# Two transformer layers on one core: the fold's slabs in buffers of their own, no fold ahead of sums that open a group, and a pause of six units behind the token split

## The chip, the cores and the metric

The kernel runs on one core of a Trainium2 chip. The metric is the device time of one execution in microseconds (us). Names of engines follow the profile: PE is TensorE (matrix products), PEld its weight loads, DVE is VectorE, ACT is ScalarE, POOL is GpSimd, and SP is SyncE, whose queue issues nearly all DMA transfers here.

## What is computed

The reference applies two blocks A and B twice, with the same weights, to 2048 tokens of 576 features in fp32. There are 32 heads of 18 features.

```python
def _A_ref(x, wq, wk, wv, wo):            # attention, one K and V for all heads
    q = (x @ wq).reshape(B, S, H, Dh).transpose(0, 2, 1, 3)
    k = x @ wk;  v = x @ wv
    p = softmax(einsum("bhqd,bkd->bhqk", q, k) * Dh ** -0.5)
    return einsum("bhqk,bkd->bhqd", p, v).transpose(...).reshape(B, S, H * Dh) @ wo

def _B_ref(x, wqkv, w_phi, wo):           # linear attention with learned features
    q, k, v = ...x @ wqkv...
    pq, pk = einsum("bhsd,hdf->bhsf", q, w_phi), einsum("bhsd,hdf->bhsf", k, w_phi)
    phi_q = concat([softmax(pq), softmax(-pq)]);  phi_k = the same of pk
    kv = einsum("bhsf,bhsd->bhfd", phi_k, v);  z = sum of phi_k over the tokens
    return ((phi_q @ kv) / (phi_q @ z + 1e-6)).reshape(B, S, D) @ wo

x = x + _A_ref(_layernorm(x), ...);  x = x + _B_ref(_layernorm(x), ...)   # twice
```

## The kernel before

The tokens are cut into 16 tiles of 128. A layer (A then B) has a **loop** in which the attention scores are computed and, beside them, most of B for the tiles that are already through A. Between the two loops, and after the second, stands a **tail** in which the rest of B is done. The first loop has work that the second lacks: the weights of B's keys and queries are first multiplied with `w_phi`, head by head, which is called the fold (`fold_phi`).

**The loop** (`attend`). A *group* is one tile of queries with half of the heads; there are 32 groups per layer. A *unit* is two score products against 128 keys (L518 on PE, into a tile `sc`) and one exponential of 1024 columns (L994 on ACT, from `sc` into `pt`). `sc` has three buffers, so PE can be three units ahead of ACT. Two units make one tile of sums (L806 on PE: `pt` times `vst`, added up over 16 tiles in an accumulator). PE runs in bursts: `scores(3)`, then either one piece of other work or two to three tiles of sums; when there is nothing else to do, the loop goes in steps of two units. Whether a piece is taken is decided while the program is written, by a credit that grows by a fixed pace per burst.

**Two accumulator banks.** One PSUM bank of the tiles `ps` and `acc` holds the running group's sums, the other one ("spare") serves all other work, one *bankful* at a time. When a group opens (its first tile of sums), the two change roles: the new sums go where the last bankful was, and the old sums are read by DVE in `finish_group` (L908, L912, L913, L916, L133, L134: six instructions in a row) before the bank can serve as spare.

**The other work** comes from the generator `stream`, by kind:
- kind F, the fold, ten slabs of `wqkv`: two sorts of transposes (L350, and L337 for the last 72 columns) that DVE copies out (L351, L338), and two sorts of products (L355, L360), which DVE copies out too (L357, L362). The slab comes by DMA (L332) into a buffer `wstage` out of three, which `load_weight` (L168, L165) uses as well for the weights that DVE splits into a high and a low part (L133, L134).
- kind P, a product of 14 matmuls (L240): two for the output projection (with `wdhi`, `wdlo`), two each for B's keys (`wahi`, called K here), values and queries. DVE evacuates a K bankful with L551 and four more instructions.
- kind U, the state update (L595, 32 small matmuls; DVE adds them with L601).

After U a tile's features are finished on DVE: `feature_end` twice (L563, L564, L565) and a transposition (L647). At the same moment the next tile's tokens are split (`turn_tokens`: L133, L134, L673, L674), and its K bankfuls may begin.

The order of PE and of DVE in the loop is the order in which the program is written (`in_order` pins it); SP's and ACT's order is chosen by the scheduler under the same dependencies. Each engine works strictly in its order.

Of the kernel before, what the change touches and what calls it, by code (L numbers as in the profile page):

```python
# [9 lines left out]
F32 = mybir.dt.float32  # L10
# [9 lines left out]
P = 128  # L20
S = 2048
D = 576
H = 32
DH = 18
NT = S // P
# [36 lines left out]
def kernel(ctx, tc, x_in, wq, wk, wv, wo, wqkv, w_phi, wob, out):  # L62
    nc = tc.nc
# [4 lines left out]
    stage = ctx.enter_context(tc.tile_pool(name="stage", bufs=3))  # L68
# [67 lines left out]
    def row_slot(src, k, cols):  # L136
        if k < 4:
            return [(slice(0, P), src[k * P : (k + 1) * P, cols])]
        return [(slice(0, 64), src[512:576, cols]), (slice(64, P), src[512:576, cols])]
# [112 lines left out]
    def bankful(kind, ps, shape=(P, HALF)):  # L252
        yield Kind(kind)
        return ps.tile(list(shape), F32, name="ps")
# [54 lines left out]
    def fold_phi(ps, tmp):  # L309
        room = tmp("bd")  # L310
        rows = room[:, : KT * DH].rearrange("p (k d) -> p k d", d=DH)
        flat = w_phi.rearrange("h d f -> (h d) f")
        nc.sync.dma_start(rows[:126, 0:4, :], flat[0:504].rearrange("(g p) f -> p g f", p=126))
        nc.sync.dma_start(rows[:72, 4, :], flat[504:576])
        bd = room[:, KT * DH : KT * 8 * DH].rearrange("p (k j d) -> p k j d", j=7, d=DH)
        for j in range(7):
            V.tensor_scalar(bd[:126, 0:4, j, :], rows[:126, 0:4, :], mask18[:126, j : j + 1],
                            None, op0=ALU.mult)
            if j < 4:
                V.tensor_scalar(bd[:72, 4, j, :], rows[:72, 4, :], mask18[:72, j : j + 1],  # L320
                                None, op0=ALU.mult)
        yield STAGE
        wt, fo = tmp("wt"), tmp("fo")
        units = [(half, k) for half in (1, 0) for k in range(KT)]

        def fetch(n):
            if n == len(units):
                return None
            half, k = units[n]
            st = stage.tile([P, D], F32, name="wstage")  # L330
            for r, part in row_slot(wqkv, k, slice(half * D, (half + 1) * D)):
                nc.sync.dma_start(st[r, :], part)  # L332
            return st

        def short(pl, st):
            if st is not None:
                T.transpose(pl[:72, :P], st[:, 504:576], idf)  # L337
                V.tensor_copy(wt[:72, 512:640], pl[:72, :P])  # L338

        st = fetch(0)  # L340
        yield STAGE
        yield STAGE
        pl = yield from bankful("F", ps, (P, P))
        short(pl, st)
        yield -110
        for n, (half, k) in enumerate(units):
            following = fetch(n + 1)
            pt = yield from bankful("F", ps, (P, 4, P))
            for g in range(4):
                T.transpose(pt[:126, g, :], st[:, g * 126 : (g + 1) * 126], idf)  # L350
            V.tensor_copy(wt[:126, 0:512], pt[:126].rearrange("p a b -> p (a b)"))  # L351
            yield -440
            po = yield from bankful("F", ps, (P, 504))
            for g in range(4):
                T.matmul(po[:, g * 126 : (g + 1) * 126], wt[:126, g * P : (g + 1) * P],  # L355
                         bd[:126, g].rearrange("p a b -> p (a b)"), start=True, stop=True)
            V.tensor_copy(fo[:, :504], po)  # L357
            yield -880
            pl = yield from bankful("F", ps, (P, 2 * P))
            T.matmul(pl[:, P : P + 72], wt[:72, 512:640],  # L360
                     bd[:72, 4, :4, :].rearrange("p a b -> p (a b)"), start=True, stop=True)
            V.tensor_copy(fo[:, 504:D], pl[:, P : P + 72])  # L362
            short(pl, following)
            nc.sync.dma_start(scratch[half, k * P : (k + 1) * P, :], fo[:, :D])
            st = following
            yield -330

    kst = const.tile([P, S], F32R, name="kst")
# [277 lines left out]
    def block_transpose(blocks, src, dst, pause=0):  # L646
        V.transpose(blocks, src)  # L647
        for _ in range(pause):
            yield
        for q in range(P // 32):  # L650
            rows = slice(q * 32, (q + 1) * 32)
            nc.sync.dma_start(dst[:, rows].rearrange("(b f) t -> f b t", f=32),
                              blocks[rows, :].rearrange("f (b t) -> f b t", t=32))
            yield
# [22 lines left out]
    def mix(i, xs, st, ps, spill, loads, slow, after):  # L677
# [7 lines left out]
        blocks = bw.tile([P, NKG, P], F32, name="pht").rearrange("p a b -> p (a b)")  # L685
        spilling = block_transpose(blocks[:, : 2 * D], eq.rearrange("p h s d -> p (h s d)"), spill[i], SPILL)
        next(spilling)
# [192 lines left out]
    def attend(layer, st, a1o, stream):  # L880
# [13 lines left out]
        with ctx1:  # L894
# [36 lines left out]
            def values(c, g, t, pt):  # L931
                if t == 0:
                    homes.reverse()
                    acc[c, g] = bank(*homes[0], [P, CW])
                add_values(acc[c, g], t, [pt[j // 2][:, j % 2, :] for j in range(GH)], t == 0, t == NT - 1)
                if t == NT - 1 and (c, g) == groups[-1]:
                    st["last"] = acc[c, g]
                elif t == NT - 1:
                    finish(c, g)
# [8 lines left out]
            def tick():  # L948
                ticks[0] += 1
                for queue in (urgent, loads, slow):  # L950
                    if queue and next(queue[0], DONE) is DONE:
                        queue.popleft()

            kind, credit, paused = [None], [0.0], [False]
# [32 lines left out]
            units = [(n, t, hh) for n in range(len(groups)) for t in range(NT) for hh in range(2)]  # L987
            pts, at, done = {}, [0], [0]
# [54 lines left out]
            def sums(until):  # L1043
                while done[0] < until:
                    n, t, _ = units[2 * done[0]]
                    values(*groups[n], t, [pts.pop((n, t, hh)) for hh in range(2)])
                    done[0] += 1
                    in_order()

            def earn(count):  # L1050
                credit[0] = min(credit[0] + st["pace"] * count / BURST, 2)

            def burst():
                ready = scores(BURST)
                tick()
                earn(BURST)
                work = peek()
                held = at[0] + BURST - 2 * done[0]
                if work == "P" and credit[0] >= 1 and not paused[0] and held <= TILES:
                    fill()  # L1060
                    credit[0] -= 1
                    paused[0] = True
                else:
                    paused[0] = False
                    if work == "F" and credit[0] >= 1:
                        fill()
                        credit[0] -= 1
                    count = 3 if credit[0] + st["pace"] >= 1 else 2
                    sums(min(ready, max(done[0] + count, -(-(at[0] + BURST - TILES) // 2))))
                    if work == "U":  # L1070
                        fill()
                    tick()

            while at[0] < len(units):
                if not st["idle"]():
                    burst()
                else:
                    ready = scores(2)
# [13 lines left out]
    BURST = 3  # L1092
    TILES = 9
    DUE = 9
    SPILL = 4
    PACES = ((0.6, 0.44), (0.39, 0.39))
    FLIP = 84
    TAIL = 100
# [18 lines left out]
    st = {"late": [], "norms": const.tile([P, NT // PAIR], F32, name="norms"), "wq": weight_tiles("b")}  # L1117
# [27 lines left out]
    with first, tc.tile_pool(name="ps0", bufs=7, space=PSUM) as ps:  # L1145
# [27 lines left out]
        pair, following = ([first_tile(i) for i in range(k, k + PAIR)] for k in (0, PAIR))  # L1173
# [46 lines left out]
    for layer in range(LAYERS):  # L1220
        last = layer == LAYERS - 1
        st.update(start_state(bw), added=set())
        with tc.tile_pool(name="a1o", bufs=2) as a1o:
# [11 lines left out]
            def stream(v, layer=layer):  # L1235
# [3 lines left out]
                unflipped, st["left"] = deque(), list(range(NT))  # L1239
                st["closed"], st["pace"] = -1, PACES[layer][0]  # L1240

                def fetch(src, i):
                    fetch_residual(src, i)
                    held.append(i)
                    spoiled.discard(i)
# [44 lines left out]
                if layer == 0:  # L1290
                    st["saves"] = [save_weight(key) for key in ("wpq", "wk", "wv")]
                st["pace"] = PACES[layer][1]
                fetched = xs = None
                weights = False

                def turn_tokens():
                    nonlocal xs, fetched
                    if fetched is not None:
                        xs = fetched[0], split_tokens(fetched[1])
                        fetched = None  # L1300

                def wanted():
                    return xs is not None and (xs[0] < st["closed"] or xs[0] == NT - 2 or v.left() < TAIL)

                def flip(i, stats):
                    nonlocal fetched
# [28 lines left out]
                while v.left():  # L1335
# [21 lines left out]
                    elif wanted():  # L1357
# [4 lines left out]
                        xs = None  # L1362
# [109 lines left out]
```

## Time and profile before

| what | us |
|---|---|
| median of 3 runs (lowest, highest) | 2712.57 (2710.81, 2718.03) |
| the profiled execution's own time | 2713.22 |
| its span in the profile | 2711.5 |
| PE busy | 2611.7 (96%) |
| ACT busy | 2148.3 (79%) |
| DVE busy | 1258.2 (46%) |
| first burst of the first loop | starts at 110.66 |
| fold, from its first PE instruction's burst to its last | 145.39 to 361.87 |
| end of the first loop's sums | about 1251.4 |

The second loop lies between about 1465 and 2567 us. In a list of waits the name on the left waited for the name on the right. In a timeline a bracket gives the idle time before the instruction and what ended it. `x16` is the number of matmul records merged into one row; a tile of sums has 8 of them, a score product 2, a P bankful 14.

### The profile page before, as it was taken

To read this page: it belongs to the slowest core of one execution; us is meant where nothing else is said; L and a number is where in the kernel's file an instruction comes from. 1 tells how busy PE (TensorE), PEld (TensorE's weight loads), DVE (VectorE), ACT (ScalarE), POOL (GpSimd) and SP (SyncE) were. 2 spreads that over 40 slices of the span, in tenths; PEclk is the share of its full clock that TensorE was granted. 3 is DMA by queue.
4 is the path that set the end of the run, shared out by engine and by line. 5 is a ranking of instruction groups with operands and counts; after the bars stand their busy time and mean duration, and the time that the engine had idled before them with its cause. 6 is when DMAs were issued, how large, how long until landed. Compare 5 with 4: busy or idle time off the path is not lost. (4 is left out here: it accounts for less than half of the span.)

```text
span 2711.5 us, 55484 instructions
## 1 busy us (share of the span) xinstructions
PE 2611.7 (96%) x22030; PEld 1450.9 (54%) x22030; DVE 1258.2 (46%) x2867; ACT 2148.3 (79%) x2511; POOL 56.8 (2%) x98
## 2 busy tenths in 40 slices
PE   7989999999999999999999999999999999999989
PEld 6633335554545544456998234444444444444588
DVE  8532245444454444445775124444444444444465
ACT  4578898888888899985334899999999999999821
POOL 1000000000000000001000000000000000000010
PEclk9989999999999999999999999999999999999999
DMA  6553243222222222223754422222222222222164
GB/s 184 172 179 124 76 140 105 59 67 59 59 59 67 57 57 59 59 48 98 234 162 146 155 60 56 58 57 57 58 57 57 57 58 57 58 58 53 43 200 144
DMA packets 476349, 245.05 MB, mean 90 GB/s; under 512 B 222706, under 2 KB 433842, under 8 KB 476082
## 3 DMA queue, kind: packets, MB, share of 16 engines
q1 hardware_dynamic: 476082, 241.41, 32.2%
q8 instruction: 177, 2.90, 0.5%
q14 instruction: 90, 0.74, 0.1%
HBM read 133.86 MB, written 105.51 MB: 88 GB/s over the span
## 5 line engine op out<-in xcount | busy, mean ns | idle before, releaser
L994 ACT ACTIVATE pt<-sc 128x1024 f32<-128x1024 f32 x2036 | 1925.3, 1047 | 222.1 <-PE sc L518 202.9
L518 PE MATMUL sc<-qst,kst 56*128 56x512 f32 x3840 | 689.4, 450 | 21.7 <-ACT pt L994 21.2
L518 PEld LDWEIGHTS sc<-qst,kst 56*128 56x128 f32 x3840 | 318.1, 185 | 534.2 <-ACT pt L994 477.3
L806 PE MATMUL acc<-pt,vst 128*32 128x512 f32 x4096 | 501.6, 603 | 4.7 <-DVE featk L357 2.4
L806 PE MATMUL ps<-pt,vst 128*32 128x512 f32 x4048 | 485.2, 603 | 5.6 <-DVE xn L351 2.7
L806 PEld LDWEIGHTS ps<-pt,vst 128*32 128x32 f32 x4048 | 110.1, 110 | 238.1 <-issue 225.2
L806 PEld LDWEIGHTS acc<-pt,vst 128*32 128x32 f32 x4096 | 106.3, 109 | 224.9 <-issue 215.3
L304 DVE TENSOR_TENSOR xc<-xc,acc 128x288 f32<-128x288 f32 x60 | 27.2, 454 | 336.8 <-PE acc L240 336.8
L240 PE MATMUL ps<-wahi,xs 128*128 128x288 f32 x801 | 175.8, 305 | 6.4 <-DVE featk L551 3.4
L240 PEld LDWEIGHTS ps<-wahi,xs 128*128 128x128 f32 x801 | 132.2, 190 | 15.2 <-DVE featk L551 4.3
L240 PE MATMUL ps<-walo,xs 128*128 128x288 f32 x445 | 131.4, 298 | 0.0
L240 PE MATMUL acc<-wdhi,on 128*128 128x288 f32 x540 | 119.4, 306 | 0.0
L240 PE MATMUL ps<-wchi,xs 128*128 128x288 f32 x495 | 109.6, 307 | 0.0
L131 ACT ACTIVATE xs<-ps 128x512 fp32r<-128x512 f32 x36 | 21.4, 595 | 109.5 <-PE ps L290 103.2
L396 PE MATMUL ps<-xsc,wbhi 128*128 128x256 f32 x576 | 107.0, 284 | 0.7 <-ACT xsc L131 0.7
L418 ACT ACTIVATE pc<-ps 128x256 fp32r<-128x256 f32 x80 | 30.4, 384 | 93.7 <-PE ps L396 93.5
L551 DVE COPY featq<-ps 128x288 f32<-128x288 f32 x47 | 21.5, 457 | 173.9 <-PE ps L240 173.8
L240 PEld LDWEIGHTS acc<-wdhi,on 128*128 128x128 f32 x540 | 88.0, 187 | 21.3 <-issue 20.9
L396 PEld LDWEIGHTS ps<-xsc,wbhi 128*128 128x128 f32 x576 | 90.9, 192 | 1.6 <-ACT xsc L131 1.1
L240 PEld LDWEIGHTS ps<-wchi,xs 128*128 128x128 f32 x495 | 81.4, 189 | 16.9 <-issue 15.4
L240 PE MATMUL acc<-wdlo,on 128*128 128x288 f32 x300 | 88.2, 294 | 0.0
L396 PE MATMUL ps<-xsc,wblo 128*128 128x256 f32 x320 | 85.8, 283 | 0.0
(260 smaller groups left out, 3056.6 us busy)
## 6 DMA issues: line engine op xcount, KB each, us to landing
qst<-qd SPq DMA_DIRECT2D x360, 72.0 KB
od<-parts SPq DMA_DIRECT2D x512, 36.0 KB
pht<-phi SPq DMA_DIRECT2D x32, 540.0 KB
qd<-pc SPq DMA_DIRECT2D x64, 256.0 KB
phi<-pht SPq DMA_DIRECT2D x112, 144.0 KB
on<-od SPq DMA_DIRECT2D x60, 256.0 KB
xd<-xc SPq DMA_DIRECT2D x32, 288.0 KB
flipped<-pht SPq DMA_DIRECT2D x112, 72.0 KB
```

The lines of the kernel that those rows point to most:

```text
L131: A.activation(dst_hi, src, AF.Copy)
L240: T.matmul(dst, xs[:, slot, :], w[half][:, k, c0 : c0 + HALF], start=(n == 0), stop=(n == last))
L304: V.tensor_add(xr, xr, po)
L396: T.matmul(po, lhs, xsc[:, slot, :], start=(n == 0), stop=(n == LASTP))
L418: A.activation(pc[:, 0, :], po, AF.Copy)
L518: T.matmul(sc, kst[head_rows(h), t * P : (t + 1) * P], q[head_rows(h), h // 2, :], start=True, stop=True)
L551: V.tensor_copy(e[:, hs, 0, :], src)
L806: T.matmul(acc[32 * j : 32 * j + 32, :], vst[:, t, :], pts[j], start=first, stop=last)
L994: A.activation(pt, sc, AF.Exp, scale=SCALE)
```

## The change

The fold's slabs get a pool name of their own (`fstage`, three buffers) and are fetched two slabs ahead instead of one; to make room for them in SBUF, the area that the program reserves for DMA descriptors is set to 1024 bytes per partition. In a burst, a piece of kind F is left out when the tiles of sums that follow it include a group's first tile; it then comes in a later burst. And a tile whose tokens have just been split may begin its K bankfuls only six units later.

```diff
         def fetch(n):
-            if n == len(units):
+            if n >= len(units):
                 return None
-            st = stage.tile([P, D], F32, name="wstage")
+            st = stage.tile([P, D], F32, name="fstage")
...
-        st = fetch(0)
+        st, following = fetch(0), fetch(1)
...
-            following = fetch(n + 1)
+            later = fetch(n + 2)
...
-            st = following
+            st, following = following, later
...
-                    if work == "F" and credit[0] >= 1:
+                    count = 3 if credit[0] + st["pace"] >= 1 else 2
+                    until = min(ready, max(done[0] + count, -(-(at[0] + BURST - TILES) // 2)))
+                    opens = any(t % NT == 0 for t in range(done[0], until))
+                    if work == "F" and credit[0] >= 1 and not opens:
                         fill()
                         credit[0] -= 1
-                    count = 3 if credit[0] + st["pace"] >= 1 else 2
-                    sums(min(ready, max(done[0] + count, -(-(at[0] + BURST - TILES) // 2))))
+                    sums(until)
...
+    SETTLE = 6
...
+                settled = 0
                 def turn_tokens():
-                    nonlocal xs, fetched
+                    nonlocal xs, fetched, settled
                     if fetched is not None:
                         xs = fetched[0], split_tokens(fetched[1])
                         fetched = None
+                        settled = v.left() - SETTLE
                 def wanted():
-                    return xs is not None and (xs[0] < st["closed"] or xs[0] == NT - 2 or v.left() < TAIL)
+                    return (xs is not None and v.left() <= settled
+                            and (xs[0] < st["closed"] or xs[0] == NT - 2 or v.left() < TAIL))
...
-    nc = _bacc.Bacc("TRN2", target_bir_lowering=False, num_devices=1)
+    nc = _bacc.Bacc("TRN2", target_bir_lowering=False, num_devices=1, dynamic_dma_scratch_size=1024)
```

What it does to the engines' order shows at three places. The first is DVE at the fold's first slab, just after the first products (L357) were copied out. `wbhi` and `wblo` are the two halves of B's value weights, of which one slab is split by each pair L133, L134. Before:

```order
L357 COPY featk<-ps 128x504
L133 CAST wbhi<-wstage 128x576
L134 TENSOR_TENSOR wblo<-wstage,wbhi 128x576
L362 COPY featk<-ps 128x72
L338 COPY xn<-ps 72x128
```

Now:

```order
L357 COPY featk<-ps 128x504
L133 CAST wbhi<-wstage 128x576
L134 TENSOR_TENSOR wblo<-wstage,wbhi 128x576
L133 CAST wbhi<-wstage 128x576
L134 TENSOR_TENSOR wblo<-wstage,wbhi 128x576
L133 CAST wbhi<-wstage 128x576
L134 TENSOR_TENSOR wblo<-wstage,wbhi 128x576
L362 COPY featk<-ps 128x72
L338 COPY xn<-ps 72x128
```

The fold has moved one to two bursts back against the splits, so that three slabs are split ahead of the copy L362 instead of one.

The second is PE behind a state update (L595) in the first loop. Before, the third one:

```order
L595 MATMUL acc<-featk,vb_1619 32x36 x32
L518 MATMUL sc<-qst,kst 128x512 x6
L240 MATMUL acc<-wahi,xs 128x288
L240 MATMUL acc<-walo,xs 128x288
L240 MATMUL acc<-wahi,xs 128x288 x2
```

Now, the second one:

```order
L595 MATMUL ps<-featk,vb_1622 32x36 x32
L518 MATMUL sc<-qst,kst 128x512 x6
L806 MATMUL acc<-pt,vst 32x512 x4
L518 MATMUL sc<-qst,kst 128x512 x4
L806 MATMUL acc<-pt,vst 32x512 x4
L518 MATMUL sc<-qst,kst 128x512 x4
L806 MATMUL acc<-pt,vst 32x512 x4
L518 MATMUL sc<-qst,kst 128x512 x6
L806 MATMUL acc<-pt,vst 32x512 x8
L518 MATMUL sc<-qst,kst 128x512 x6
L240 MATMUL ps<-wahi,xs 128x288
```

Between the update and the K bankful (`wahi`) there are now two steps of two units and a burst with sums alone.

The third is DVE at the first loop's end, where the tail begins with the copy of the last group's sums (L861), its reciprocals (L868) and their spread (L870). Before:

```order
L565 TENSOR_TENSOR featq<-featq,fz 128x576
L647 STREAM_TRANSPOSE pht<-featq 128x1152
L861 COPY osb<-acc 128x512
L868 RECIPROCAL rd<-ps 128x16
L870 COPY wide<-rd 128x512
```

Now:

```order
L861 COPY osb<-acc 128x512
L563 TENSOR_REDUCE fz<-featq 128x32
L601 TENSOR_TENSOR kv<-kv,ps 128x288
L564 RECIPROCAL fz<-fz 128x32
L565 TENSOR_TENSOR featq<-featq,fz 128x576
L868 RECIPROCAL rd<-ps 128x16
L647 STREAM_TRANSPOSE pht<-featq 128x1152
L870 COPY wide<-rd 128x512
```

The last mixed tile's features are now finished between L861 and L870: the loop's last bursts hold its last query bankful and its update, where before there were eight steps of two units.

## The prediction

> **What bounds the kernel now.** The page first: its span and its costliest group.
>
> ```profile
> span 2711.5 us, 55484 instructions
> ...
> L994 ACT ACTIVATE pt<-sc 128x1024 f32<-128x1024 f32 x2036 | 1925.3, 1047 | 222.1 <-PE sc L518 202.9
> ```
>
> ACT's exponentials are the longest group, but ACT sits idle for 222 us ahead of them, nearly all of it until PE has the scores. So PE, which carries all other products too, ends most waits, and ACT ends them only where PE has little else. Next the busy times of three stretches: the fold, the rest of the first loop, and most of the second loop.
>
> ```profile
> 145.39:361.87 216.48, 196.23 (x1341) 80.62 (x1338) 55.97 (x106) 173.64 (x185) 0.00 (x0) 0.94 0.39 123
> 361.87:1251.40 889.53, 871.94 (x7254) 437.93 (x7250) 422.90 (x853) 794.20 (x863) 8.12 (x15) 0.99 0.27 68
> 1500.00:2567.40 1067.40, 1057.38 (x8582) 500.83 (x8574) 437.65 (x879) 987.69 (x1069) 8.09 (x15) 1.00 0.24 62
> ```
>
> The columns are the length, the busy time of PE, PEld, DVE, ACT and POOL, and the granted clock. In the fold PE is idle for 216.48 - 196.23 = 20 us, and a clock of 0.94 means 0.06 x 216 = 13 us lost; in the rest of the loop 17.6 us and 0.99; in the second loop 10 us of a longer stretch and 1.00. What the change can win lies in these idle times and in what hangs on them. Who ended PE's waits in the fold, and in the rest of the loop (us in total, times, longest):
>
> ```profile
> PE ps L337 <- DVE featk L362: 5.6, 6, 2.5
> PE ps L806 <- DVE xn L351: 2.7, 1, 2.7
> PE acc L806 <- DVE featk L357: 2.4, 1, 2.4
> PE acc L806 <- DVE xn L338: 2.0, 1, 2.0
> ```
>
> ```profile
> PE ps L240 <- DVE featk L551: 3.4, 2, 1.7
> PE ps L240 <- DVE turned L908: 2.6, 4, 1.2
> PE ps L806 <- DVE featk L551: 2.5, 2, 2.3
> ```
>
> PE waits for copies that DVE owes it; no transposition of the fold waited for its slab. Hence fetching two slabs ahead removes no wait by itself. What it changes is who holds the `wstage` buffers.
>
> **Sums that open a group.** The first of three cases:
>
> ```profile
> 149.11 0.28 DVE L338 COPY xn<-acc 72x128 f32<-72x128 f32 x1
> ...
> 149.45 2.38 PE L806 MATMUL acc<-pt,vst 128*32 128x512 f32 x16 [1.98 <-DVE xn L338]
> ```
>
> A fold bankful sits in the bank that the new group needs, and its copy stands on DVE behind `finish_group` of the old group. The three single waits above, 2.0 + 2.4 + 2.7 = 7.1 us, are of this sort, and the new rule leaves none: -7.1. Some may come back one burst later, where a moved piece's copy L362 stands behind the same six DVE instructions and holds L337; the order shows that at one place, and I add +1 (0 to 2.5, L337's longest wait).
>
> The longest of the three also shows what follows a wait:
>
> ```profile
> 335.55 1.94 PE L806 MATMUL ps<-pt,vst 128*32 128x512 f32 x8 [2.75 <-DVE xn L351]
> 337.41 1.65 PE L518 MATMUL sc<-qst,kst 56*128 56x512 f32 x6
> 338.99 3.35 PE L806 MATMUL ps<-pt,vst 128*32 128x512 f32 x16
> ...
> 344.26 1.06 PE L806 MATMUL ps<-pt,vst 128*32 128x512 f32 x8
> 345.25 1.03 PE L518 MATMUL sc<-qst,kst 56*128 56x512 f32 x6
> ```
>
> Behind 2.75 us of idling, rows of one shape take nearly twice their time: (1.94 - 1.06) + (1.65 - 1.03) + (3.35 - 2 x 1.06) = 2.7 us. This wait cost 5.5 us in all. The Trainium skill ("TensorE: Matmul & The Clock Gate", "Why this matters for your kernels") asks only that PE have no idle gap of more than about 3 us between bursts, as one idle window takes the clock to half. By that, waits of 2 to 2.75 us would cost no clock. The rows above disagree, so I price the clock from them; what the rule would make of the sum stands with the rivals.
>
> **The weight splits.** The other waits of the fold, DVE's and PE's rows:
>
> ```profile
> 163.83 0.46 DVE L133 CAST wbhi<-wstage 128x576 fp32r<-128x576 f32 x1 [5.73 <-DMA wstage<-in_B_wqkv_dram]
> 164.32 0.76 DVE L134 TENSOR_TENSOR wblo<-wstage,wbhi 128x576 fp32r<-128x576 f32 x1
> ...
> 165.28 0.43 PE L337 MATMUL ps<-idf,wstage 128*72 128x128 f32 x1 [1.74 <-DVE featk L362]
> ...
> 185.51 0.43 PE L337 MATMUL ps<-idf,wstage 128*72 128x128 f32 x1 [2.51 <-DVE featk L362]
> ```
>
> L337 waits for the copy L362, which stands behind a split, which waits for its slab. At 185.51 it is the next matrix; there the new order puts fewer splits ahead of the copy, and that wait goes: -2.5. At 165.28 it gets worse, since three slabs are now split ahead of L362 instead of one. The first cannot land much before 163.83, because the ten saves that SP issues ahead of it stay. Three splits of 0.46 + 0.76 us and their gaps, 1.25 each, end at 163.83 + 3.75 = 167.6; with the copy, L337 starts at about 168. Now it is ready at 165.28 - 1.74 = 163.5, and with the first wait of 1.98 us gone some 1.7 us earlier, 161.8. That is a wait of 6.2 us for 1.74: +4.5. The bounds are 0 (the slabs land early) and +23 (each waits as long as the first did, a rival below); I take the value nearest to the row. SP also issues the first reads of the folded matrix (L165) among the fold now, as their buffers are free; each waits there for a write of that slab. Behind them stand queries needed a group, 32 units, later: zero while that cover holds; beyond it PE's scores would wait by as much.
>
> The clock: 2.7 us for the third opening, and as much for the wait at 185.51 by analogy; nothing for the rest: -5.4 (between 0 and the 13 us). **Fold: -7.1 + 1 - 2.5 + 4.5 - 5.4 = -9.5 us.** It ends with the same unit as before, so equal numbers of bursts are compared.
>
> **The pause behind the split.** K's first bankful ran at once behind the split, and its copy L551 stands on DVE behind the last tile's features, so the next user of the bank waits. That chain is made of
>
> ```profile
> L565 DVE TENSOR_TENSOR featk<-featk,fz 128x576 f32<-128x576 f32 x28 | 21.2, 758 | 1.0
> ...
> L563 DVE TENSOR_REDUCE fz<-featk 128x32 f32<-128x576 f32 x28 | 20.8, 743 | 0.0
> L564 DVE RECIPROCAL fz<-fz 128x32 f32<-128x32 f32 x56 | 19.8, 353 | 1.9
> L647 DVE STREAM_TRANSPOSE pht<-featq 128x1152 f32<-128x1152 f32 x14 | 19.3, 1379 | 0.5
> ```
>
> 2 x (743 + 353 + 758) + 1379 ns = 5.1 us, no longer than six units at ACT's pace (below). So the waits for L551 go: -(3.4 + 2.5) = -5.9. K's weight loads also waited for the split itself:
>
> ```profile
> PEld ps L240 <- DVE xs L134: 1.8, 5, 0.4
> ```
>
> -1.8. The waits for L908 stay. Clock: three of the removed waits, at a third of the 2.7 and a little more: -3 (0 to -4.5, half of the 0.01 x 889 us). At two tiles an output bankful now comes right behind the update and may meet the same chain: +1. **Rest of the loop: -5.9 - 1.8 - 3 + 1 = -9.7 us.**
>
> **What the pause costs.** ACT's sixteen exponentials at the first loop's end, then PE's rows of one two-unit step there:
>
> ```profile
> 1235.50 14.78 ACT L994 ACTIVATE pt<-sc 128x1024 f32<-128x1024 f32 x16
> ```
>
> ```profile
> 1236.55 0.73 PE L518 MATMUL sc<-qst,kst 56*128 56x512 f32 x4
> 1237.21 1.07 PE L806 MATMUL acc<-pt,vst 128*32 128x512 f32 x8
> 1238.21 0.74 PE L518 MATMUL sc<-qst,kst 56*128 56x512 f32 x4
> ```
>
> ACT needs 14.78 / 16 = 0.92 us a unit, 1.85 a step (and 5.5 for six units); PE alone takes 1238.21 - 1236.55 = 1.66. A step loses 0.19. The order has 40 such steps for 33: the pauses are mostly paid by the eight steps at the end, which disappear. 7 x 0.19 = 1.3, and with a last burst that now holds a bankful, **+2** (0 to 6).
>
> At the start of the tail L563, L601, L564, L565 and L647 now stand between L861 and L870, and PE's next product needs L870. L601's length is that of the second loop's row:
>
> ```profile
> 2559.19 0.45 DVE L601 TENSOR_TENSOR kv<-kv,ps 128x288 f32<-128x288 f32 x1 [1.13 <-PE ps L595]
> ```
>
> 0.74 + 0.45 + 0.35 + 0.76 + 1.38 = 3.7 us; part of it falls beside PE's own transpositions, so 3, and 1.5 for the clock behind it: **+4.5** (2 to 6.5). In the second loop the last update moves back by seven units, and DVE's chain behind it, 5.1 + 0.45 us, outlasts a closing burst of three units by about a microsecond: **+1**. The smaller descriptor area touches no instruction: zero.
>
> **Sum:** -9.5 - 9.7 + 2 + 4.5 + 1 = -11.7 us. The profiled execution's own time is 2713.2 us, 0.65 above the median of the three runs: 2713.2 - 11.7 = **2701.5**. With its bounds the case runs from 2694 to 2707.
>
> **Rivals.**
> - *The half clock stays* (0.20). It falls behind the waits that remain, and the removed ones give back only themselves: without -5.4 and -3 the sum is -3.3, 2709.9. For it: one wait becomes longer and the tail has a new one. Against it: the second loop, with hardly a wait, has 1.00. By the skill's rule the tail's 1.5 us would go as well, giving 2708.4; the trace speaks against the rule, as said.
> - *The splits do not hold PE* (0.17). All three slabs land early; the 4.5, the 1 and the tail's 1.5 us vanish: -18.7, 2694.5. Against it stands DVE's measured wait of 5.73 us.
> - *Slower: the splits hold PE for good* (0.14). DVE waits 5.73 us not for the first slab alone but for each of the next two, and for the two of the second matrix that now stand ahead of L357: 4 x 5.73 = 23 us in place of nothing, with fold copies behind every one. -11.7 + 23 = +11, 2724.5. It decides as soon as these four waits exceed 11.7 us together. For it: the saves and slabs share one queue, and the fold now fetches more ahead. Against it: the fold moves 123 GB/s (last column of its row) with engines busy 0.39, so the queue drains.
>
> The forecast has 0.49. A measurement of this kernel can tell about 0.3%, 8 us, from no change, so below 2704.5 is faster: 0.40 of the forecast's chance, the second rival's 0.17 and 0.03 of the first make 0.60; 0.26 lie within; 0.14 above. The range of 2691 to 2714 leaves out the slower rival and a little at the bottom.
>
> **What would show it.** In the profile after: no wait of L806 for L338, L351 or L357; one wait of L337 for L362 of some 6 us near 168; a clock above 0.94 in the fold; a fold about 10 us shorter; no waits of L240 for L551; a wait of about 3 us of L873 for L870 at the first tail. I am wrong if the fold is not shorter by at least 5 us, or if the stretch behind it is longer than before.

## The result, and the profile after

The changed kernel takes 2721.08 us (median of 7 runs, 2719.48 to 2725.35), the kernel before 2713.86 on the same chip (7 runs). The ratio is 1.0029, with a 95% interval of 1.0017 to 1.0040: slower by some 7 us, where the prediction said 2701.5 and a range up to 2714. The profiled execution took 2723.35 us, 2721.6 of it the span; that is 10.1 us more than the profiled execution before, so the stretches below add up to 10 us and not to 7.

The page hardly shows it: the costliest group is the same, and ACT waits less for PE than before.

```profile
span 2721.6 us, 55456 instructions
...
L994 ACT ACTIVATE pt<-sc 128x1024 f32<-128x1024 f32 x2036 | 1925.1, 1046 | 209.9 <-PE sc L518 188.6
```

So the program is cut at five points that both kernels have: the fold's end, the first L864 (transposition of the last group's sums, the loop's end), the second loop's first score, the second L864, and the end. First the busy times of the changed kernel's five stretches (length; PE, PEld, DVE, ACT, POOL; granted clock; DMA share, GB/s), then of the last three in the kernel before:

```profile
145.40:357.81 212.41, 191.59 (x1340) 80.77 (x1336) 56.17 (x106) 173.73 (x185) 0.00 (x0) 0.97 0.39 124
357.81:1239.09 881.28, 869.02 (x7254) 436.37 (x7251) 421.78 (x852) 794.94 (x863) 8.12 (x15) 1.00 0.27 68
1239.09:1482.11 243.02, 218.86 (x2303) 210.45 (x2304) 163.41 (x487) 72.32 (x170) 20.64 (x30) 0.94 0.55 163
1482.11:2572.70 1090.59, 1072.77 (x8638) 506.75 (x8638) 439.48 (x887) 1000.13 (x1082) 8.11 (x15) 0.99 0.25 64
2572.70:2721.59 148.89, 136.28 (x1604) 129.91 (x1604) 85.61 (x244) 25.47 (x58) 10.43 (x10) 0.94 0.54 161
```

```profile
1252.23:1480.10 227.87, 217.55 (x2303) 208.46 (x2304) 161.62 (x484) 72.62 (x170) 20.64 (x30) 0.97 0.56 169
1480.10:2568.16 1088.06, 1071.44 (x8637) 505.73 (x8637) 439.38 (x887) 1000.06 (x1082) 8.09 (x15) 0.99 0.25 65
2568.16:2711.45 143.29, 129.31 (x1604) 123.60 (x1604) 85.71 (x244) 24.89 (x58) 10.43 (x10) 1.00 0.54 164
```

The first loop ends 13.1 us sooner, at 1239.09 for 1252.23. The stretch between the loops then takes 243.0 us for 227.9, so the second loop starts 2.0 us later than before. It is 2.5 us longer, and what follows it 5.6 (how far these two are the change's is told at the end). Between the loops PE does the same work, but idles 243.02 - 218.86 = 24.2 us for 10.3. Who ended its waits there (us in total, times, longest), in the changed kernel:

```profile
PE ps L757 <- DMA wbhi<-wqd: 10.1, 1, 10.1
PE ps L757 <- DMA pht<-phi: 5.6, 1, 5.6
...
PE ps L873 <- DVE wide L870: 1.6, 1, 1.6
PE ps L864 <- DVE kv L601: 1.3, 1, 1.3
```

L757 are the first products of the second pass over the tiles. They need `pht`, a tile's query features, which the loop stored in `phi` and which are read back. The first two tiles on PE in the changed kernel, and the first three in the kernel before:

```profile
1291.45 2.58 PE L757 MATMUL ps<-kvb,pht 108*64 108x57 f32 x44 [10.12 <-DMA wbhi<-wqd]
1303.18 2.58 PE L757 MATMUL ps<-kvb,pht 108*64 108x57 f32 x44 [5.57 <-DMA pht<-phi]
```

```profile
1294.49 1.48 PE L757 MATMUL ps<-kvb,pht 108*64 108x57 f32 x44 [0.61 <-DMA kvb<-featk]
1302.36 2.43 PE L757 MATMUL ps<-kvb,pht 108*64 108x57 f32 x44
1309.19 1.48 PE L757 MATMUL ps<-kvb,pht 108*64 108x57 f32 x44
```

PE was ready at 1281.3 and started at 1291.45; after both waits rows of the same shape take 2.58 us instead of 1.48, the half clock (0.50 in the rows of 1285 to 1295 further below). The kernel before has one slow row too, 2.43 us, in 5 us with a clock of 0.55. (The first wait is put down to a weight, `wbhi`, which L757 doesn't use; it is the transfer that landed nearest. PE's weight loads of the same line name `pht<-phi`.) Why `pht` comes late is read from SP's queue behind the loop, first of the kernel before, then of the changed one (start, time, line, transfer):

```profile
1237.84 3.54 SPq L652 DMA_DIRECT2D phi<-pht  x4
1244.29 0.30 SPq L643 DMA_DIRECT2D pht<-phi  x1
1256.25 3.86 SPq L838 DMA_DIRECT2D od<-parts  x8
...
1271.52 0.40 SPq L643 DMA_DIRECT2D pht<-phi  x1
...
1280.95 0.34 SPq L203 DMA_DIRECT2D wahi<-wobd  x1
...
1290.28 2.63 SPq L745 DMA_DIRECT2D kvb<-featk  x3
```

```profile
1241.53 0.32 SPq L652 DMA_DIRECT2D phi<-pht  x1
1244.01 4.29 SPq L838 DMA_DIRECT2D od<-parts  x8
...
1251.36 1.93 SPq L652 DMA_DIRECT2D phi<-pht  x3
...
1269.88 0.34 SPq L203 DMA_DIRECT2D wahi<-wobd  x1
...
1278.53 2.65 SPq L745 DMA_DIRECT2D kvb<-featk  x3
...
1283.24 0.40 SPq L643 DMA_DIRECT2D pht<-phi  x1
...
1285.32 0.44 SPq L203 DMA_DIRECT2D wbhi<-wqd  x1
```

Before, the last mixed tile's features were stored (L652) while the loop still ran; their buffer, the one that tile 0's read needs, was free at 1244, and two reads (L643) went out ahead of the reload of 20 weights (L203). Now three of the four stores go out at 1251.36, behind the last group's parts, and the first read stands behind ten of the weights, 39 us later than before. From 1285 us on the DMA engines are full, as the changed kernel's rows show:

```profile
1270.00:1280.00 10.00, 8.26 (x120) 7.70 (x120) 6.11 (x14) 2.03 (x4) 3.10 (x4) 1.00 0.53 179
1280.00:1285.00 5.00, 1.32 (x10) 1.09 (x9) 4.22 (x10) 1.36 (x2) 1.02 (x1) 0.91 0.67 169
1285.00:1290.00 5.00, 0.00 (x0) 0.00 (x0) 0.49 (x2) 0.00 (x0) 1.30 (x2) 0.50 0.98 241
1290.00:1295.00 5.00, 3.55 (x49) 3.48 (x50) 1.40 (x6) 0.00 (x0) 0.00 (x0) 0.50 1.06 374
```

In the kernel before they are about as full (0.94 to 1.04 in four of the five stretches of 5 us from 1280 to 1305), but there the reads of the first two tiles went out ahead of the weights, and PE doesn't wait for them.

### The profile page after: what moved, and what is told of

The parts are those of the page before. It is cut to its first block, busy times and chain, and to the rows that moved or that the text cites. A ratio compares the mean times of both kernels' runs of the same rounds, so it can differ in the third digit from the quotient of the medians.

```text
span 2721.6 us, 55456 instructions
## 1 busy us (share of the span) xinstructions
PE 2614.0 (96%) x22030; PEld 1459.1 (54%) x22030; DVE 1258.3 (46%) x2867; ACT 2149.4 (79%) x2511; POOL 56.8 (2%) x98
## 5 line engine op out<-in xcount | busy, mean ns | idle before, releaser
L240 PE MATMUL ps<-wahi,xs 128*128 128x288 f32 x810 | 178.8, 307 | 1.0 <-ACT xs L131 0.6
L240 PEld LDWEIGHTS ps<-wahi,xs 128*128 128x128 f32 x810 | 135.8, 192 | 8.0 <-issue 3.9
L240 PE MATMUL ps<-walo,xs 128*128 128x288 f32 x450 | 133.6, 299 | 0.0
L240 PE MATMUL acc<-wdhi,on 128*128 128x288 f32 x540 | 120.8, 309 | 2.7 <-DMA on<-od 2.5
L240 PE MATMUL ps<-wchi,xs 128*128 128x288 f32 x486 | 107.0, 306 | 0.0
L240 PEld LDWEIGHTS acc<-wdhi,on 128*128 128x128 f32 x540 | 88.5, 189 | 25.1 <-issue 21.5
L551 DVE COPY featq<-ps 128x288 f32<-128x288 f32 x46 | 21.0, 458 | 153.0 <-PE ps L240 152.5
L240 PE MATMUL acc<-wdlo,on 128*128 128x288 f32 x300 | 88.7, 296 | 0.0
L240 PEld LDWEIGHTS ps<-wchi,xs 128*128 128x128 f32 x486 | 79.3, 188 | 16.9 <-issue 16.1
L240 PEld LDWEIGHTS ps<-walo,xs 128*128 128x128 f32 x450 | 86.6, 192 | 0.0
```

The source lines that it names most:

```text
L240: T.matmul(dst, xs[:, slot, :], w[half][:, k, c0 : c0 + HALF], start=(n == 0), stop=(n == last))
L551: V.tensor_copy(e[:, hs, 0, :], src)
```

## The experiments

Ratios are to the kernel before on the same chip, each from 11 or 12 runs of the edited kernel (5 for the second) and 29 to 35 of the kernel before. The stretches are cut from each run's one profiled execution, at the same rows as above.

**Which edit costs?** The first takes the pause back (`SETTLE = 0`), the second keeps it alone:

```
-    SETTLE = 6
+    SETTLE = 0
```

> The changed kernel with the pause taken back (0 units), fold edits kept. Theory A (the pause lets the last tiles' features be stored after the first loop, so that the first reads of them stand behind the reload of weights on SP's queue; the fold edits bring what they show at the end of the fold, some 4 us): the last group of the first loop starts some 4 us ahead of before, the first reads stand ahead of the weights again, the 10 us wait of L757 is gone, and the time is 2707 to 2711 us. Theory B (what lies between the loops is bound by the weights' transfers, whatever the pause, so a loop that ends sooner only waits longer there): L757 waits for what the loop gained, and the time is 2713 to 2715 us. Theory C (the loss comes from the fold edits): 2718 us or more.

Measured: 2711.12 us, ratio 0.9995 (0.9985 to 1.0004). The time is 10 us less than the changed kernel's and, with 1 inside the interval, not told from the kernel before. The loop ends at 1248.2, 228.1 us lie between the loops, and L757 waits 0.3 us, for `kvb`.

The second has the fold as in the kernel before (the smaller descriptor area stays):

```
-            st = stage.tile([P, D], F32, name="fstage")   # and the other fold lines of the diff
+            st = stage.tile([P, D], F32, name="wstage")
-                    if work == "F" and credit[0] >= 1 and not opens:
+                    if work == "F" and credit[0] >= 1:
```

> The kernel before with the pause of 6 units alone, no fold edit. Theory A: the first loop gains some 9 us behind the fold, then loses some 15 us between the loops, 2.5 in the second loop and 6 behind it: 2713.9 - 9 + 23.5 = 2728 us, with the 10 us wait of L757 for a read of the features. Theory B: L757 waits for the weights as long as the loop gained; the second loop and its tail lose 8: 2720 to 2723 us. Theory C: 2713 to 2716 us.

Measured: 2728.45 us, ratio 1.0054 (1.0042 to 1.0067), the time that A gave, by somewhat other parts: the loop ends at 1244.0, 8.2 us sooner, and 247.5 us lie between the loops, 19.6 more than before where A had 15. L757's waits there:

```profile
PE ps L757 <- DMA pht<-phi: 17.6, 2, 10.5
```

The pause alone makes the kernel slower; theory C is out. B is out as well in the form it had: without the pause a loop that ends 4 us sooner starts the next one 4 us sooner (1476.3).

**Can a shorter pause keep the gain?**

```
-    SETTLE = 6
+    SETTLE = 3
```

> The changed kernel with a pause of 3 units in place of 6. With 3 the first two reads of the features stand ahead of the weights on SP's queue, as before the change. Theory A: nothing of the loss between the loops is left; the fold's 4 us and most of the loop's 9 stay: 2701 to 2707 us. Theory B: 2713 to 2716 us. Theory C: 2718 us or more.

Measured: 2715.28 us, ratio 1.0005 (0.9995 to 1.0016), a miss for A. Between the loops it takes 229.7 us, as A said; but the loop gains nothing, 1250.0. Three units are too few, and one wait for L551 is now longer than any before:

```profile
PE ps L806 <- DVE featk L551: 6.1, 1, 6.1
PE ps L240 <- DVE featk L551: 3.4, 2, 1.7
```

**Is it the second loop's pause as well?**

```
-                        settled = v.left() - SETTLE
+                        settled = v.left() - (0 if layer else SETTLE)
```

> The changed kernel with the pause of 6 units in the first loop only. Theory A (the loss comes from the pause, at the ends of the loops, each end by itself): the first loop and its end as in the changed kernel, the second loop starting at 1482 us; from there as in the run without a pause, 232 us to the end: 2713 to 2716 us, some 7 less than the changed kernel. Theory D (the second loop and the end lose because the half clock and the waits between the loops carry on): 2720 us or more, as the changed kernel.

Measured: 2721.18 us, ratio 1.0023 (1.0013 to 1.0033), as the changed kernel. A missed: the pause in the second loop costs nothing that can be measured. Nor are the 5.6 us behind the changed kernel's second loop the pause's: by its rows above PE idles less there than before (12.6 us for 14.0), and the clock is 0.94 for 1.00. The same stretch took 143.5 us in the first run and 149.9 and 150.8 in two others without a pause. D isn't shown by this; that stretch differs from run to run with its clock.

**Does the place on SP's queue cost?** First the weights' reload starts two stages later, which puts both reads ahead of it:

```
-    PREP = 1
+    PREP = 3
```

> The changed kernel, pause of 6 kept; the reload of the weights behind each loop starts two stages later, so that the first two reads of the features stand ahead of it on SP's queue. Theory A: the 10 us wait of L757 and the 5 us one behind it go, and nothing waits for the later weights: 6 to 10 us less than the changed kernel, 2711 to 2715 us. Theory B: the weights are what is waited for, so later weights cost more: 2722 us or more.

Measured: 2716.11 us, ratio 1.0008 (0.9997 to 1.0018), 5 us better than the changed kernel and 1 us above A's range. L757 starts at 1281.3, but later tiles wait 8.3 us for their features: 238.1 us between the loops. So neither theory is met. Then the reads come first and the weights stay:

```
+            first_phts = {}
+            for i in (0, 1):
+                first_phts[i] = room(i)
+                load_features(first_phts[i], spills[layer], i)
             if not last:
                 reload_w4(sp)
...
-                pht = room(i)
-                load_features(pht, spills[layer], i)
+                pht = first_phts.get(i)
+                if pht is None:
+                    pht = room(i)
+                    load_features(pht, spills[layer], i)
```

> The changed kernel, pause of 6 in both loops; the reads of the features of the first two tiles are issued first thing behind a loop, ahead of the reload of w4 and of the ten or twenty weights, and not among them. Theory A (the place of the reads on SP's queue is what costs): L757 starts at about 1281 us without a wait for a transfer, the second loop at 1467 to 1470 us for 1482, and the end gains as well: 2703 to 2709 us. Theory B (the sum of the transfers between the loops bounds that stretch, in whatever order): L757 waits later, at the third or fourth tile, the second loop starts at 1477 us or later as with later weights: 2712 to 2718 us.

Measured: 2717.77 us, ratio 1.0010 (1.0000 to 1.0020), as B said. The first two reads go out at 1259.80, 23 us sooner than in the changed kernel, so their buffer was free by then and only the order on SP's queue had kept them back. The first tile starts at 1281.9 as A said, but the wait has moved to the third, which shares its buffer with the first and whose read stands behind the 20 weights:

```profile
PE ps L757 <- DMA pht<-phi: 10.4, 1, 10.4
```

The same with the pause in the first loop only, and without a pause:

> The run before (reads first) with the pause in the first loop only. Theory A: 2698 to 2703 us, faster than both kernels. Theory B: 2706 to 2712 us.

> The changed kernel without a pause and with the two reads first. There they stand ahead of the weights in any case, so under theory A moving them brings nothing: 2709 to 2713 us, as without a pause (2711). If the early reads are a gain of their own that has nothing to do with the pause (theory E): 2706 us or less.

Measured: 2717.10 us, ratio 1.0009 (0.9997 to 1.0020), and 2711.52 us, 0.9990 (0.9980 to 1.0000). Without a pause nothing is gained beyond the first run, as A and B alike would have it. With it the time lies above the ranges of both, and A is wrong, since reads that come first don't bring the time back. In the run with the reads first SP issued one weight at 1268.99 and then stood until 1277.64 at the stores into `kvb`:

```profile
1268.99 0.34 SPq L203 DMA_DIRECT2D wahi<-wobd  x1
1277.64 2.64 SPq L745 DMA_DIRECT2D kvb<-featk  x3
1280.38 0.48 SPq L203 DMA_DIRECT2D walo<-wobd  x1
```

So the next run puts the weights ahead of these stores as well, by priority:

```
+            with tc.high_priority():      # around the two reads and reload_w4
...
+                with tc.high_priority():
                     run(load("wob", "a", wob, slice(0, D), engines=(A, V)))
```

> As the run with the reads first and the pause in the first loop only; the reads, w4 and all ten loads of the output weights also get a higher priority, which puts them ahead of the three stores into kvb on SP's queue, where 9 of the 10 stood behind them and SP waited from 1269.3 to 1277.6 us with the DMA engines at 0.14. Theory B' (from 1281 us on the transfers bound the stretch, and what counts is how much SP issued before): the weights end some 6 us sooner, the third tile's L757 starts at 1295 to 1299 us for 1304 to 1306, the second loop at 1468 to 1472 us for 1478, and the time is 2705 to 2710 us. Theory F (the chain through the last group and kvb is what ends last, not the transfers): the third tile starts as late as there, 2715 to 2718 us.

> The same places on SP's queue without any pause. There 9 of the 10 loads and both reads stood ahead of the stores into kvb already, so by theory B' little is left to gain: 2708 to 2712 us (2711 without a pause, as built). By theory F: 2711 as well. If the early transfers gain as much here as with the pause, the pause has no part in it: 2705 us or less.

Measured: 2709.72 us, ratio 0.9985 (0.9974 to 0.9996), and 2709.57 us, 0.9981 (0.9971 to 0.9992). Both are faster than the kernel before, by 0.15 and 0.19%, with intervals that end below 1. The first meets what B' gave as its time, but not its steps: the third tile starts at 1301.5 and the second loop at 1474.0, since L757 still waits 4.4 us for features and 3.2 for `kvb`. Without a pause the stretch takes 226.1 us for 234.7: the pause ends the loop 5.7 us sooner and starts the next one 2.9 us later.

**The transfers themselves.** Three runs leave out the low halves of the two weights reloaded behind the loop; GpSimd writes zeros there.

```
         for n, (tile_, kept) in enumerate(pieces(st[key], wd[key])):
-            nc.sync.dma_start(tile_, kept)
+            if n % 2 and key in ("wob", "wq"):
+                G.memset(tile_, 0.0)
+            else:
+                nc.sync.dma_start(tile_, kept)
```

> The changed kernel without the low halves of the output weights and of the next layer's query weights: 10 of the 20 loads between the loops (2.9 of 5.9 MB) and 5 of the 10 behind the second loop are left out, and GpSimd fills their places with zeros. Theory B' (the transfers bound what lies between the loops): the weights end some 8 us sooner, L757 waits 0 to 4 us for 16, the second loop starts at 1468 to 1475 us for 1482, and the time is 2707 to 2713 us. Theory F (the chain through the last group and kvb): the second loop starts at 1479 us or later, 2717 us or more.

> The same left out of the kernel before. Its L757 waits hardly 2 us for transfers, so by theory B' little is to be gained: the second loop starts 1 to 4 us sooner than its 1480, 2709 to 2713 us. By theory F nothing changes: 2713 to 2715 us.

> The same left out of the run with all transfers early and the pause in the first loop only. Theory B': the rest of its wait goes, the second loop starts at 1466 to 1470 us for 1474, 2701 to 2706 us. Theory F: 1474 and 2709 to 2711 us.

Measured: the changed kernel so lightened 2712.17 us, ratio 0.9989 (0.9978 to 1.0000), with 232.4 us between the loops for 243.0; the kernel before 2715.74 us, 1.0001 (0.9989 to 1.0012), 230.2 for 227.9; the run with all early 2708.51 us, 0.9977 (0.9967 to 0.9986), 228.1 for 234.7. L757's waits in the first of them (its line is 760 there, three lines were added):

```profile
PE ps L760 <- DMA pht<-phi: 2.0, 1, 2.0
PE ps L760 <- DMA kvb<-featk: 0.2, 1, 0.2
```

With half the weights, the two waits of 15.7 us shrink to 2.2, and the stretch loses 10.6 of its 15.1 extra us; the kernel before gains nothing by the same. This fits B' and rules F out for the changed kernel: the transfers are what is waited for, and only where the pause has been put in. It doesn't show whether that is the number of bytes or the place on the queue, since fewer loads also move the reads: they still stand behind the output weights, but those are now five, and the first read goes out at 1272.78 us for 1283.24. Two expectations failed. The kernel before was to start its second loop 1 to 4 us sooner and to take 2709 to 2713 us, and starts it at 1479.8 for 1480.1. And the last of the three takes 2708.5 us for 2701 to 2706, though its second loop starts at 1469.7 as expected.

**The fold's two edits.** The slab buffers alone, then the rule on openings alone, both without a pause:

> Of the change only the folded slabs' own buffers, fetched two ahead; folds stand ahead of values that open a group as before, no pause. By the terms of the prediction: the wait at 185.51 goes (-2.5), the one of L337 near 168 grows (+4.5), the openings stay: the fold ends some 2 us later than before or as before, 2713 to 2717 us. Rival (the whole gain of the fold is the buffers): fold 2 to 4 us shorter, 2710 to 2712 us.

> Of the change only the rule that no fold stands ahead of values that open a group; slabs as before, no pause. By the terms of the prediction: the openings go, -7.1 + 1 and part of the half clock: the fold 6 to 9 us shorter, 2705 to 2708 us. Rival (the waits at the openings only move to a later burst): the fold as long as before within 2 us, 2712 to 2715 us.

Measured: 2710.12 us, ratio 0.9990 (0.9980 to 1.0001), and 2713.67 us, 0.9998 (0.9986 to 1.0009). Both times fall in the rivals' ranges and not in those of the prediction's terms, and neither is told from no change. Both keep the smaller descriptor area, and there is no sign that it costs anything. The rule alone is worth nothing that can be measured, and its waits show why: the openings are gone, but L337's waits grew.

```profile
PE ps L337 <- DVE featk L362: 9.1, 6, 6.0
PE acc L337 <- DVE featk L362: 2.4, 3, 1.8
PE acc L240 <- DMA on<-od: 2.2, 2, 1.4
```

So it is the rule, and not the slabs' buffers, that makes the long wait of L337: 6.0 us with the rule alone, at most 2.5 with the buffers alone, and 4.6 in the changed kernel with both.

Last, the kernel before with all transfers early and no edit of the change:

> The kernel before, without any edit of the change, with the reads, w4 and the ten output weights put early as in the runs with all transfers early. If the early transfers gain by themselves some 2 us and the fold edits some 2 us (the run without a pause 2711, with all early 2709.6): 2711 to 2713 us. If the fold edits carry all of it: 2713 to 2715 us.

Measured: 2714.68 us, ratio 0.9998 (0.9989 to 1.0006). The early transfers gain nothing there; together with the fold edits they gain 0.19% (0.9981). The intervals of these two runs just overlap, so how the 0.19% divide is left open.

## Why the prediction was wrong

**Up to the loop's end it was off by 4 us, and partly right by luck.** Fold, rest of the loop and pause were to bring -9.5 - 9.7 + 2 = -17.2 us at L864 (the tail's +4.5 falls almost wholly behind that row). The trace has -13.1.

- *The fold* (-9.5) brought -4.1: 212.41 us for 216.48. By the prediction's own sign (at least 5 us) that was too little. First two of PE's waits in the kernel before, beside those that the prediction shows; then who ended its waits in the changed kernel:

```profile
PE sc L518 <- ACT pt L994: 6.5, 21, 0.4
PE acc L337 <- DVE featk L362: 1.0, 3, 0.3
```

```profile
PE sc L518 <- ACT pt L994: 8.5, 27, 0.4
PE ps L337 <- DVE featk L362: 7.7, 6, 4.6
PE acc L337 <- DVE featk L362: 2.5, 3, 1.8
PE acc L240 <- DMA on<-od: 2.2, 2, 1.5
```

The openings' 7.1 us are gone, as said, and L337 waits 4.6 us, ending at 167.34 (6.2 and 168 were said). But PE's idle time, 20.3 us before, is 20.8: the waits of L337 grew by 3.6 us in all where +3 were counted (-2.5 + 4.5 + 1; two new ones of 1.8 us stand at 189.50 and 299.80), an output bankful now waits 2.2 us for its heads, and scores wait for ACT (8.5 us for 6.5), neither of which was counted. What the fold won is the clock, 0.97 for 0.94: PE's busy time fell by 4.6 us here, and over the profiled runs it is 192.4 us on average with both edits and 195.2 without, so some 3 us of the -5.4 are borne out. The failed term is "-7.1": it took removed waits for won time. Over the runs, the fold ends at 357.8 to 361.0 with both edits (mean of 12 profiled runs 359.3) and at 360.8 to 362.3 without (mean of 4, 361.5), so the edits are worth some 2 us.

- *The rest of the loop* (-9.7, with +2 for the pause) came out at -9.1 for -7.7: 881.3 us from the fold's end to L864 for 890.4. The waits of L240 for L551 are gone as said, those for L908 too (0.5 left of 2.6), which were to stay. The -1.8 were waits of weight loads; PE's own list has none for `xs`. The -3 for the clock is at least partly luck: PE's busy time fell by 2.9 us, but two runs without a pause have 867.8 and 867.9 us there, less than the changed kernel's 869.0. What the pause shows in all its runs is less idling: 11.9 to 12.5 us, for 18.4 to 19.1 without. All eight runs with a pause of 6 and the trace of the changed kernel have 880.7 to 881.8; those without have 886.6 to 890.4.

- *The tail* (+3 and 1.5 for the clock): L864 and L873 wait 2.9 us for 1.1, so +1.8 of the +3; L873's wait for L870 is 1.6 us, where 3 were said.

**Between the loops it was wrong.** The step that failed is the one on the tail's start. It counted the five DVE instructions of the last tile that now stand behind the loop, and stopped there: it left out the four stores L652 that SP issues behind the last of them, the reads L643 that need the same buffer, and what SP's queue puts ahead of those. Apart from that start, the prediction gave the stretch no term. It took 15.1 us more. The runs showed in the term's place: the pause moves the last tile's features past the loop's end, the reads fall among the reload of the weights, the DMA engines are full from 1285 to 1305 us (shares of 0.93 to 1.06), and PE waits 15.7 us and runs at half clock behind each wait. The loop ended sooner, but the last tile's features did not: their L647 runs at 1240.18, where it ran at 1236.43 before. The order of DVE now, and the row before:

```profile
1239.33 0.76 DVE L565 TENSOR_TENSOR featq<-featq,fz 128x576 f32<-128x576 f32 x1
1240.01 0.25 DVE L868 RECIPROCAL rd<-ps 128x16 f32<-128x16 f32 x1
1240.18 1.33 DVE L647 STREAM_TRANSPOSE pht<-featq 128x1152 f32<-128x1152 f32 x1
```

```profile
1236.43 1.38 DVE L647 STREAM_TRANSPOSE pht<-featq 128x1152 f32<-128x1152 f32 x1
```

**Behind it**, the second loop's +1 was 2.5 in the trace, and the 5.6 us at the end had no term; the run with the pause in the first loop only says that neither is the pause's by more than a measurement can tell. Over the profiled runs the second loop takes 1089.6 us on average with its pause of 6 (5 runs, 1088.4 to 1090.6) and 1088.0 without any (12 runs, 1086.5 to 1089.1), so the +1 is about right; the end takes 144.5 to 148.9 us and 142.7 to 150.8, which doesn't tell the two apart.

**The rivals.** The slower one came true by its sign but not by its mechanism: L337 waits 4.6 us once, not 23. What decided was a fourth case, of which nothing was said. (The second rival's -18.7 also dropped the tail's 1.5 us, with which the slabs have nothing to do; without that it is -17.2.) Without the low halves the stretch keeps 4.5 us over the kernel before (232.4 for 227.9), but only 2.2 over that kernel with the same loads left out (230.2); how much of this is L864's and L873's waits and how much the clock is open.

## What to carry to other kernels

A step that is moved past a loop's end takes its stores with it, and with them every read that needs their buffer: follow the buffer on the DMA queue to the first instruction that waits for the read, and only then call the step moved. A stage that ends sooner may win nothing if the transfers that the next stage waits for come no sooner. Waits that are removed are won time only if the engine's idle time in that stretch falls: add up the idle time, not the removed waits.

## What was not expected of the hardware

The time of one and the same kernel follows the granted clock: over the runs of the kernel before, 2708.9 us on average at 0.989 (10 runs), 2714.2 at 0.985 (34) and 2720.8 at 0.982 (7). So a change of 3 us is settled by medians of many runs, not by a profile. The end behind the second loop shows it, where the same products take PE 129.3 us at a clock of 1.00 and 136.3 at 0.94; when that happens wasn't found in the waits ahead of it. And the place of a read on a queue mattered where the DMA engines were full: PE waited 15.7 us for reads that stood among twenty weight loads, and 2.2 us with half of the loads left out. The Trainium skill ("Trainium Kernel Development and Optimization", "Key Constraints") says that issuing from several engines only saves issue time, as all share the same 16 DMA engines. The rows with a share of 0.98 and 1.06 agree in that the transfers, not SP's issuing (some 0.4 us each), were the limit there; issuing from another engine was not tried.
